# Tuned attention and MoE kernel: activation sums for two groups at a time in tiles 3 to 6, and another written order of tiles 1 to 6

## The chip, the cores and the metric

The kernel runs on one core of one Trainium2 chip. The metric is the device time of one execution in microseconds (us). Three runs of the kernel before gave 268.6, 267.94 and 268.05 us, so its median is 268.05 us. The profile was taken in one more execution of 268.22 us.

Five engines work side by side, each through a list of instructions of its own, in the order of that list: TensorE (PE; its weight loads are PEld), VectorE (DVE), ScalarE (ACT), GpSimd (POOL) and SyncE (SP), which here only issues DMAs. An instruction starts when the engine is free and the semaphores that it waits for have come.

## The reference, cut to what matters

Linear attention is followed by a two-layer network with a leaky ReLU:

```python
q_s = exp(q - max(q, axis=-1)); q_s = q_s / sum(q_s, axis=-1)      # q, k, v: (8, 8, 576, 64)
k_s = exp(k - max(k, axis=2));  k_s = k_s / sum(k_s, axis=2)
kv  = einsum('bhsd,bhse->bhde', k_s, v)
x   = einsum('bhsd,bhde->bhse', q_s, kv)                           # as (4608, 512)
h   = x @ w_in                                                     # w_in: (512, 2048)
out = maximum(0.01 * h, h) @ w_out                                 # w_out: (2048, 512)
```

## The kernel before, in words

The 4608 rows of x are nine tiles of 512 rows (tiles 0 to 8), and they come from eight batches of 576 rows (batches 0 to 7). Batch b has to be through the attention before the tile that uses its rows begins. So the attention of a batch runs beside the network of an earlier tile.

**Layer 1.** In tiles 1 to 5 it is a plain product: a word `u` in the order makes 4 matmuls, weights from `w_in_sb`, into a bank of PSUM (`ph`, line 516), and a word `l` lets ACT take the bank through the leaky ReLU into `gj` (line 525). In tiles 6 to 8 it is a scheme with seven products (`m1` to `m7`, line 918) where ACT and DVE take sums in between.

**Layer 2.** From tile 1 on it has seven products (`P1` to `P7`, line 948, bank `acc`) instead of eight. Four of them need sums of activations instead of activations: `n0` to `n3`, differences made on DVE (line 1005) and kept in the tiles `gs`. `P5` needs `n0`, `P6` needs `n1`, `P7` needs `n2` and `P3` needs `n3`; `n1` and `n3` are made from `n0` and `n1`. The activations of a tile stand in four groups p = 0 to 3. In the tiles named in `PAIRED`, one DVE instruction makes a sum for two groups (a half of the tile, 1024 elements to a partition); in the others there is one for each group (512 elements). In `PAIRED = (1, 2)` these are tiles 1 and 2; tiles 3 to 8 go by single groups. Between the products ACT copies a bank aside (`q1`, `q5`, `q6`: line 1015), and DVE adds it back at the end (`d11`, `d12`, `d22`: line 897). `w0` and `w1` issue the stores of a finished half tile on SP.

**The attention of a batch b.** `lk`, `lq`, `lv` issue loads on SP. `kt`, `km` take the maximum of k (DVE), `ks` subtracts it (DVE for batches 2 to 4, else POOL, line 193), `ke` takes exp (ACT, line 201), `va`, `vb` cast v (ACT, line 211), `kv` multiplies on PE (line 294), `kr` and `kd` scale the result. `qm` takes the maximum of q (DVE), `qs` subtracts it (POOL, line 256), `qe` takes exp (ACT, line 264), `qu` sums (DVE, line 273), `qn` divides (DVE, line 280), `qt` issues on SP a DMA that transposes (`qX`, line 457). Then `A` multiplies on PE (`po`, line 438), and `x` lets ACT copy a bank of that into `xT` (line 429), from which `u` or `m` read.

**What sets the order.** After tile 0 all of this is written out by hand, or by a search of its author, as one list of words, `SCORE`, which is played from left to right by `play`. Each word appends its instructions to the lists of its engines. The order of words therefore is the order on every engine, on SP's DMAs and POOL too; how far one engine runs ahead of another is left to the semaphores. A word that begins with a digit belongs to that tile: `5P200` is product 2 of tile 5, first block of 128 rows, first half of the sum, 4 matmuls; `5n0_1` is the second sum `n0` of tile 5. In the others the digit behind the letters is the batch: `A6.1` is the second part of `A` for batch 6, and `x6.10` copies the first of its two banks; `qn2.1` is the second part of the rows of batch 2. `SCORE` covers tiles 1 to 6 and batches 2 to 7. Tile 0 and batches 0 and 1 stand ahead of it, and tiles 7 and 8 follow it, in an order of their own (`WEAVE`). PSUM has six banks in the pool `psB` (`ph`, `po`, part of `acc`) and two in `psO`; a bank is given to the next user in turn once its last reader is through.

Line numbers are those of the kernel before. In the changed kernel all lines behind `SCORE` are two lower (948 is 946, 1005 is 1003, 1015 is 1013).

Of the kernel before, what the change touches and what calls it, by code (L numbers as in the profile page):

```python
# [25 lines left out]
def kernel(  # L26
# [759 lines left out]
    def xsums(t, steps=slice(0, 4)):  # L786
# [13 lines left out]
        1u13 1u02 kt2.1 kt2.2 kt2.3 1u00 1u01 1l00 1l02 1l13 1u03 1l03 lk3 1u06 1u10 qm2.1 qs2.1 qm2.0 1l01  # L800
        km2 lq3 1l06 qe2.1 qu2.1 1u04 1l04 1l10 1u12 1u07 ks2 qs2.0 qe2.0 qu2.0 1l12 1l07 1u11 1u15 1P100
        1l11 1u17 1n0_0 va2 1u05 1l05 1u14 1u16 1P101 1n1_0 ksB2 1l15 1l14 1l17 1l16 1P110 1P111 1P200 1n0_1
        1q1 qn2.0 1P201 qt2.0 1n1_1 qn2.1 qt2.1 1P500 1P501 1P510 1P511 1n2_0 1P600 1P601 1P610 1P611 T3
        1P210 vb2 1n2_1 1P211 lv3 1n3_0 ke2 kv2 1q6 1P700 1P701 kr2 1q5 1P710 1P711 1P300 lq4 1n3_1 1P301
        1d11 kd2 A2.0 x2.01 A2.1 x2.10 x2.00 x2.11 A2.2 kt3.0 1P310 1P311 1d22 1P400 1P401 kt3.1 kt3.2 x2.20
        1P410 qm3 1P411 x2.21 2u06 kt3.3 2u02 va3 vb3 2u04 2l04 2l06 km3 2u00 2l00 2u01 lq6 2l02 2l01 2u03
        1q21 qs3 2l03 qm4 lk5 2u17 qe3 2l17 2u10 2l10 2P100 2u07 2l07 ks3 1d12 2u12 lk4 2u05 2l05 2u14 2l12
        2u13 2u16 1w1 2l13 2u11 2u15 2P101 2l16 2l11 qs4 qu3 2P110 ksB3 2l14 2P111 2P200 2l15 qn3 2P201 ke3
# [1 line left out]
        2n2_0 qt3 2P510 2P511 kt4.0 2n2_1 2d11 2P700 lv4 2P701 2P710 A3.0 kt4.1 A3.1 2q5 2n3_0 qe4 x3.10  # L810
        A3.2 2P711 2P300 2n3_1 2P301 2P310 x3.01 2P311 kt4.2 2d22 x3.21 2P400 2P401 2P410 kt4.3 km4 ks4
        x3.20 2P411 x3.11 x3.00 3u06 3u04 3u17 2q21 3u15 3u07 va4 3l04 vb4 3l06 3l17 ksB4 3l15 3l07 3u00
        3l00 3u02 3u01 ke4 kt5.0 kt5.1 kt5.2 kt5.3 km5 ks5 3u13 3u11 kv4 3l02 3l13 3l01 3l11 3u05 3l05 kr4
        3u16 2d12 3u10 kd4 lv6 3u03 3l03 lq5 qu4 3l16 3u12 qn4 3l12 3n0_1 3u14 3l14 lk6 3n0_3 3l10 3n0_0
        3n0_2 3n1_1 3n3_1 lv5 va5 3P100 3P101 3P110 3P111 3q1 3P200 3P201 3P210 3P211 2w1 3P500 3P501 vb5
        qt4 3n1_2 3P510 3P511 3n1_0 3n1_3 3n3_0 2w0 3n3_2 3P600 3P601 3P610 3n2_3 3q5 3n3_3 3P611 3n2_1 3d11
        ke5 3P300 3q6 kt6.0 3P301 3P310 A4.0 A4.1 3n2_0 A4.2 kv5 kt6.1 3n2_2 kt6.2 lq7 qm5 3P311 3P700 x4.01
        x4.00 lk7 x4.20 kt6.3 3P701 3P710 3P711 x4.11 x4.21 x4.10 4u13 3d12 va6 4u02 4l02 4u12 4u03 3d22 vb6
        3P400 3P401 qs5 3P410 3P411 kr5 kd5 4l13 4u07 4l03 4l12 km6 4u06 4u00 4u17 qe5 4l06 4l17 qu5 4l07
# [10 lines left out]
        6m1_1 X6.0 Z0 X6.1 X6.2 5P710 5P210 X6.3 Z1 5P711 5d22 qe7 6s1_1 4w1 5P211 5d11 6m5_1 kd7 qu7 qn7  # L830
        6m1_2 6s1_2 5P400 5P401 5P410 5P411 5q21 6m1_0 6s1_0 Z2 6m1_3 6m6_1 6m6_2 6s1_3 6s6_1 6s6_2 6m6_0
        6m2_1 6c11_1 6m7_1 6s6_0 6s5_1 6m5_2 6s5_2 5P301 5P310 5P311 6l11_1 6c22_1 6m6_3 6l22_1 6m3_1 5d12
        6m4_1 6c12_1 6m2_2 6m3_2 6m2_3 6s6_3 6c11_2 6l21_1 6l12_1 qt7 6c11_3 6l11_2 6m5_3 6m5_0 6s5_3 6s5_0
        6m2_0 6c11_0 6m7_3 6l11_3 6c22_3 6m7_2 6c22_2 6l11_0 6m7_0 6l22_3 6m3_3 6m3_0 6c22_0 6m4_3 6l22_2
# [310 lines left out]
```

## Time and profile before

| | us |
|---|---|
| median of three runs (267.94 to 268.6) | 268.05 |
| profiled execution, its own time | 268.22 |
| span of its trace | 266.4 |
| PE busy (96%) | 256.3 |
| DVE busy (84%) | 224.6 |
| ACT busy (72%) | 193.0 |
| POOL busy (24%) | 64.3 |

The span goes from the first instruction to the last; 1.8 us of the execution's own time lie around it. The busy time of PE counts matmuls with modelled ends, so that it tells whether PE ever waited, and not how fast it went; how fast it went is to be read from the time that a number of equal matmuls took. The chain of waits is followed back from the last instruction, and its pieces are given in the order of time: start, length, engine, tile and line, and how many instructions. The view of groups gives, by line and shape, how many instructions there are, their busy time, and the mean of one.

### The profile page before, as it was taken

The page shows a single profiled execution, that of the slowest core. Times are in us where ns is not written, and L with a number is a line of the kernel's source. Part 1 is how long each engine was busy: PE and PEld are TensorE (multiplying, and loading weights), DVE is VectorE, ACT ScalarE, POOL GpSimd, SP SyncE. Part 2 cuts the span into 40 slices and gives each one's busy share as a digit, 9 for nine tenths or more (in the row PEclk, how much of TensorE's full clock was granted, in tenths as well). Part 3 has the DMA queues.
Part 4 walks back from the last instruction along what each step waited for, and adds up shares of the span by engine and source line. Part 5 has one row for each costly group of instructions (what it writes and reads, how often), then busy time and mean ns, then how long its engine had stood idle before and what let it go on. Part 6 is the DMA issues. An engine that isn't in the chain of part 4 may idle for free.

```text
span 266.4 us, 6323 instructions
## 1 busy us (share of the span) xinstructions
PE 256.3 (96%) x2570; PEld 188.6 (71%) x2570; DVE 224.6 (84%) x390; ACT 193.0 (72%) x367; POOL 64.3 (24%) x45
## 2 busy tenths in 40 slices
...
PEclk9999999999999999999999999999999999999999
...
GB/s 228 349 211 355 319 211 276 321 309 259 181 397 391 179 264 347 181 258 147 310 72 27 229 93 2 31 209 11 17 209 25 14 184 41 2 88 72 1 2 159
DMA packets 37646, 46.49 MB, mean 174 GB/s; under 512 B 18160, under 2 KB 21232, under 8 KB 37616
## 3 DMA queue, kind: packets, MB, share of 16 engines
...
## 4 chain that ended last, share of the span: by engine, by line
PE 85%; DMA 6%; ACT 2%; DVE 1%; issue 0%; POOL 0%; ACTq 0%; POOLq 0%
PE acc L948 37%; PE ph L516 29%; PE ph L918 14%; DMA w_in_sb<-in_moe_w_in_dram 3%; DMA qX<-qe 3%; PE po L438 2%; PE pkv L294 1%; ACT ke L201 1%; DVE k_raw L380 1%; PE pout L541 1%; PE po L294 1%; ACT vb L211 1%; ACT qe L264 0%; POOL w_in_sb L129 0%; DVE out_sb L897 0%
## 5 line engine op out<-in xcount | busy, mean ns | idle before, releaser
L516 PE MATMUL ph<-xT,w_in_sb 128*128 128x256 bf16 (+3 forms) x512 | 86.0, 326 | 0.5 <-DMA w_in_sb<-in_moe_w_in_dram 0.5
L516 PEld LDWEIGHTS <-w_in_sb 128*128 128x128 bf16 x512 | 49.7, 98 | 33.0 <-DMA w_in_sb<-in_moe_w_in_dram 0.8
L525 ACT ACTIVATE gj<-ph 128x512 bf16<-128x512 f32 (+2 forms) x116 | 60.7, 579 | 14.8 <-PE ph L516 11.7
L948 PEld LDWEIGHTS <-gs 128*128 128x128 bf16 x512 | 49.5, 98 | 6.2 <-issue 0.4
L256 POOL TENSOR_TENSOR q_raw<-q_raw,qmax 128x2304 f32<-128x2304 f32 (+3 forms) x10 | 31.0, 3104 | 62.5 <-DVE qmax L225 48.8
L948 PEld LDWEIGHTS <-gj 128*128 128x128 bf16 x384 | 37.4, 98 | 6.3 <-issue 0.5
L948 PE MATMUL acc<-w_out_sb,gj 128*128 128x256 bf16 x256 | 32.2, 273 | 0.0
L948 PE MATMUL acc<-w_out_sb,gs 128*128 128x256 bf16 x256 | 30.8, 273 | 0.0
L948 PE MATMUL acc<-wsum,gs 128*128 128x256 bf16 x256 | 29.9, 273 | 0.0
L897 DVE TENSOR_TENSOR part_spare<-ph,part_spare 128x512 f32<-128x512 f32 x36 | 23.8, 686 | 3.9 <-PE ph L918 3.6
L1005 DVE TENSOR_TENSOR gs<-gj 128x512 bf16<-128x512 bf16 (+1 forms) x56 | 24.3, 455 | 2.0 <-ACT gj L525 1.6
L429 ACT CAST xT<-po 128x512 bf16<-128x512 f32 (+3 forms) x47 | 19.0, 486 | 9.3 <-PE po L438 9.2
L982 ACT COPY part_spare<-ph 128x512 f32<-128x512 f32 x36 | 19.5, 594 | 8.3 <-PE ph L918 8.0
L1005 DVE TENSOR_TENSOR gs<-gj,gs 128x512 bf16<-128x512 bf16 (+1 forms) x56 | 24.1, 458 | 0.5
L280 DVE TENSOR_TENSOR qe<-qe,qrec 128x2304 bf16<-128x2304 bf16 (+4 forms) x12 | 23.7, 1973 | 0.2
L273 DVE TENSOR_REDUCE qsum<-qe 128x36 f32<-128x2304 bf16 (+4 forms) x11 | 19.7, 1793 | 4.6 <-ACT qe L264 4.6
L1015 ACT COPY keep<-acc 128x512 f32<-128x512 f32 x22 | 12.8, 588 | 11.7 <-PE acc L948 11.7
L193 POOL TENSOR_TENSOR k_raw<-k_raw,kall 128x2304 f32<-128x2304 f32 x3 | 15.2, 5064 | 24.2 <-DVE kall L185 24.2
L897 DVE TENSOR_TENSOR out_sb<-acc,keep 128x512 f32<-128x512 f32 (+1 forms) x26 | 16.4, 642 | 5.0 <-PE acc L948 3.7
L918 PEld LDWEIGHTS <-fs_spare 128*128 128x128 bf16 x192 | 18.8, 98 | 2.2
L225 DVE TENSOR_REDUCE qmax<-q_raw 128x36 f32<-128x2304 f32 (+4 forms) x11 | 19.5, 1790 | 0.4 <-DMA q_raw<-in_q_dram 0.4
L918 PE MATMUL ph<-xs_spare,fs_spare 128*128 128x256 bf16 x144 | 19.0, 273 | 0.0
...
## 6 DMA issues: line engine op xcount, KB each, us to landing
...
```

What stands on the lines that cost most here:

```text
L225: nc.vector.tensor_reduce(out=m, in_=st[b]["q"][:, :, rs], axis=AX.X, op=ALU.max)
L256: eng.tensor_tensor(out=qs, in0=qs, in1=st[b]["qmax", rs.start].unsqueeze(3).to_broadcast([P, HL, n, D]), op=ALU.subtract,)
L273: nc.vector.reduce_sum(out=qsum, in_=st[b]["qe"][:, rs], axis=AX.X)
L280: eng.tensor_tensor(out=qes, in0=qes, in1=st[b]["qrec", rs.start].unsqueeze(3).to_broadcast([P, n, HL, D]), op=ALU.mult,)
L429: eng.copy(out=o, in_=i)
L516: nc.tensor.matmul(ph[:, n0:n1], lhsT=w_in_sb[:, i, j * P : (j + 1) * P], rhs=xT[:, i, (c0 + n0) % NX : (c0 + n0) % NX + n1 - n0], start=( ...
L525: nc.scalar.activation(out=o, in_=ph, func=AF.Prelu, alpha=LEAKY_SLOPE)
L897: nc.vector.tensor_tensor(out=o, in0=x, in1=y, op=ALU.add)
L918: nc.tensor.matmul(bank[x, t, p][:, jj], lhsT=lhs(k, 2 * p + jj), rhs=rhs[:, k], start=(first and k == 0 and jj == 0), stop=(k == 1), skip ...
L948: nc.tensor.matmul(b[:, at_], lhsT=lhs(k)[:, sub * P : (sub + 1) * P], rhs=rhs[:, k], start=(first and k == 0 and at_ == 0), stop=(k % (NK ...
L982: nc.scalar.copy(out=fill(t, kind, p), in_=bank["Z" if kind == "s5" else "X", t, p])
L1005: nc.vector.tensor_tensor(out=o, in0=x, in1=y, op=ALU.subtract)
```

## The change

1. `PAIRED` takes in tiles 3 to 6. There the sums `n0` to `n3` are made for a half tile each: 8 instructions of 1024 elements in a tile, in place of 16 of 512. The code for it (`corners`, `place`) was there for tiles 1 and 2.
2. `SCORE` is another list. It has 699 words in place of 731: the 32 words of single sums that fall away are `n0_2`, `n0_3` and so on in tiles 3 to 6; all other words are the same, in another order.

Nothing else differs. Which engine does which work, the products, the loads, the stores, tile 0, and tiles 7 and 8 are as before.

```diff
-    PAIRED = (1, 2)
+    PAIRED = (1, 2, 3, 4, 5, 6)
     SCORE = """
...
-        2n0_0 2P210 2n0_1 2P211 2n1_0 2n1_1 2P500 kv3 2q1 2P600 2P601 2P610 2P611 2q6 kr3 kd3 1w0 2P501
...
-        4q1 4P510 4n2_0 4P600 4n3_3 4P601 4P610 4P611 ke6 4P511 4q6 4n3_2 kt7.1 A5.0 x5.01 A5.1 x5.00 4n2_1
-        A5.2 kv6 x5.20 x5.21 kt7.2 4n3_1 4n3_0 4n2_3 4n2_2 4P700 4P701 4P710 4P711 qm6 4q5 4P300 qm7 x5.10
-        x5.11 4P301 4P310 4P311 4d22 4P200 4P201 kr6 kd6 4P210 qs6 qs7 kt7.3 qe6 5u02 5l02 4P211 4P400 4P401
...
-        5q1 3w1 5n1_0 5n3_0 5P500 5n1_2 5P501 5P510 5P511 5P600 5P601 F1 ke7 5q5 A6.0 x6.01 A6.1 x6.00 F3
-        5n3_2 A6.2 kv7 5P610 5P611 x6.11 F2 F4 5q6 5n3_3 5P200 x6.20 5P300 5P201 5P700 5P701 x6.21 kr7 x6.10
...
-        6c12_3 6n1_1 6l12_0 6n0_0 6n1_0 6l12_2 6n0_2 6l12_3 6n0_3 6n2_3 A7.0 x7.00 A7.1 x7.11 6P210 6n1_3
...
-        6w0 A7.2 x7.20 6P400 6P401 6P410 x7.21 X7.0 X7.1 X7.2 6P411 6q21 6w1 X7.3 5w0
...
+        1l17 1l03 1u14 1l14 1u16 1l16 ksB2 1P100 qu2.0 qn2.0 1P101 1P110 1P111 1P200 ke2 1P201 1P210 1n0_0
+        1n0_1 qn2.1 1P500 1P501 1P510 1n1_0 lq3 1n1_1 1P211 va2 qt2.0 1q1 1P511 1P600 vb2 1q5 1n3_0 kv2
+        1P601 qt2.1 1P300 1n2_0 kr2 1P610 1P611 1n3_1 1P301 1d11 kd2 A2.0 A2.1 A2.2 1P310 1q6 x2.01 x2.00
...
+        2n2_0 kd3 2P601 kt4.0 kt4.1 2P610 2q5 2P611 lk6 A3.0 A3.1 2n3_1 A3.2 2q6 2P300 x3.20 x3.10 x3.01
...
+        3u05 3u14 3l05 kv4 kr4 kd4 3l14 3P100 3u13 3l13 3u15 3u16 3l16 qn4 lq6 3P101 3P110 lv6 3l15 3P200
+        2w0 qt4 3P111 3P201 3n0_0 3n0_1 3P210 3P211 3n1_1 3n1_0 3P500 3P501 3P510 3P511 3q1 3P600 3n3_1
...
+        4P610 4P611 4q6 qt5 A5.0 A5.1 A5.2 4q5 x5.10 kv6 qm6 x5.11 x5.01 3w0 qs6 4P700 4P701 4P710 4P711
+        x5.00 x5.21 4P300 4P301 4P310 4d22 km7 x5.20 4P200 4P201 4P210 va7 vb7 kr6 kd6 4P400 4P401 4P211
+        4P410 4P411 5u00 5l00 5u02 5l02 5u01 5l01 qe6 4d11 5u06 ks7 4P311 F1 qm7 5u12 qs7 5u07 5l06 5l07
+        4q21 qu6 4w1 4d12 5l12 5u03 5l03 5u10 ke7 5u05 5u04 5l04 5u16 qn6 3w1 5l10 5l16 5l05 5u13 5l13 5u15
+        5u11 5l11 5u17 5l17 5n0_0 5u14 5n2_0 5l15 5P100 5P101 5P110 5P111 5n2_1 5l14 5n0_1 5P500 5P501 5q1
+        5P510 5n1_0 5P600 5n1_1 5P601 5P610 5n3_1 5P611 5q6 qt6 A6.0 x6.00 A6.1 x6.10 A6.2 F2 x6.01 kv7
+        x6.20 5P200 x6.21 5P511 x6.11 5P700 5q5 qe7 5P701 5P201 5P210 5P710 5P211 5P711 F3 F4 5n3_0 X6.0 Z0
...
+        6n1_1 6P600 6P501 6P510 6l21_3 6P601 6P610 6l21_2 6n2_0 6P611 A7.0 A7.1 6q6 A7.2 6P511 x7.20 6P700
```

More of the change, by code (lines that the diff above doesn't have):

```diff
@@ L799 @@
     SCORE = """
[L800 to L808, printed above, removed]
-        2n0_0 2P210 2n0_1 2P211 2n1_0 2n1_1 2P500 kv3 2q1 2P600 2P601 2P610 2P611 2q6 kr3 kd3 1w0 2P501
@@ L810 @@
[L810 to L819, printed above, removed]
@@ L820 @@
-        4n0_1 4u04 4l00 ks6 qn5 4u16 4l16 kt7.0 4u01 4l01 4n0_3 4n1_3 3q21 4u14 4l04 4u11 4l11 4u05 4l05
-        4u10 4u15 4l10 4n0_0 4n1_0 4l15 4P100 4P101 qt5 4l14 4n0_2 4n1_2 4P110 4P111 4n1_1 4P500 4P501 lv7
-        4q1 4P510 4n2_0 4P600 4n3_3 4P601 4P610 4P611 ke6 4P511 4q6 4n3_2 kt7.1 A5.0 x5.01 A5.1 x5.00 4n2_1
-        A5.2 kv6 x5.20 x5.21 kt7.2 4n3_1 4n3_0 4n2_3 4n2_2 4P700 4P701 4P710 4P711 qm6 4q5 4P300 qm7 x5.10
-        x5.11 4P301 4P310 4P311 4d22 4P200 4P201 kr6 kd6 4P210 qs6 qs7 kt7.3 qe6 5u02 5l02 4P211 4P400 4P401
@@ L825 @@
-        3w0 4P410 va7 km7 4P411 5u01 5u06 5l06 5u04 5u00 5l00 5l01 4d11 5u16 vb7 5u10 5l04 qu6 4d12 5l16 ks7
-        5u11 qn6 5u17 5l10 4q21 5l11 5n0_0 5l17 5u03 5l03 5u12 5u05 5l05 5n2_2 5l12 5u13 5l13 5n0_1 5n1_1
-        5P100 5n3_1 5u07 5l07 5n0_3 qt6 5u15 5n2_3 5n2_1 5l15 5u14 5l14 5n1_3 5n0_2 5n2_0 5P101 5P110 5P111
-        5q1 3w1 5n1_0 5n3_0 5P500 5n1_2 5P501 5P510 5P511 5P600 5P601 F1 ke7 5q5 A6.0 x6.01 A6.1 x6.00 F3
-        5n3_2 A6.2 kv7 5P610 5P611 x6.11 F2 F4 5q6 5n3_3 5P200 x6.20 5P300 5P201 5P700 5P701 x6.21 kr7 x6.10
@@ L830 @@
[L830 to L834, printed above, removed]
@@ L835 @@
-        6c12_0 6l21_3 6m4_2 6l21_2 6c12_2 6m4_0 6l22_0 6P100 6P101 6P110 6P111 6l21_0 6P200 6P201 6n0_1
-        6c12_3 6n1_1 6l12_0 6n0_0 6n1_0 6l12_2 6n0_2 6l12_3 6n0_3 6n2_3 A7.0 x7.00 A7.1 x7.11 6P210 6n1_3
-        6q1 6n3_1 x7.10 6P500 6P501 6n2_0 6P510 6n1_2 6P511 6q5 6n2_1 6P600 6P601 6n3_2 6n3_0 6P610 6n3_3
-        6P611 4w0 6P211 6q6 6n2_2 6P300 6P301 6d11 x7.01 6P700 6P701 6P710 6P711 6P310 6P311 5w1 6d22 6d12
-        6w0 A7.2 x7.20 6P400 6P401 6P410 x7.21 X7.0 X7.1 X7.2 6P411 6q21 6w1 X7.3 5w0
+        1u00 1l00 1u11 1u10 1l10 1l11 1u02 1u04 1u15 kt2.1 kt2.2 kt2.3 1u05 qm2.1 1u12 1l02 qs2.1 qm2.0 1u07
@@ new lines @@
+        1l04 1l15 km2 1u06 qe2.1 1l05 1u13 1l12 qu2.1 qs2.0 qe2.0 1u03 ks2 lk3 1l13 1u01 1l06 1l07 1l01 1u17
+        1l17 1l03 1u14 1l14 1u16 1l16 ksB2 1P100 qu2.0 qn2.0 1P101 1P110 1P111 1P200 ke2 1P201 1P210 1n0_0
+        1n0_1 qn2.1 1P500 1P501 1P510 1n1_0 lq3 1n1_1 1P211 va2 qt2.0 1q1 1P511 1P600 vb2 1q5 1n3_0 kv2
+        1P601 qt2.1 1P300 1n2_0 kr2 1P610 1P611 1n3_1 1P301 1d11 kd2 A2.0 A2.1 A2.2 1P310 1q6 x2.01 x2.00
+        1P311 x2.20 T3 lq4 1P700 1n2_1 x2.21 1P701 lv3 1P710 1P711 x2.11 kt3.0 kt3.1 kt3.2 kt3.3 qm3 x2.10
@@ new lines @@
+        2u02 2l02 2u12 2l12 2u03 2l03 2u06 2u00 qs3 1d22 1P400 1P401 1P410 va3 vb3 2l00 2l06 qm4 qe3 km3
+        1d12 2u14 lk4 1w0 1P411 qs4 2u04 2l04 2u13 2l14 2u01 2l01 2u11 2u07 2l13 qu3 lv4 2u15 2u05 2l11 1q21
+        2l05 2l15 2u17 2l17 2l07 ks3 2u10 2l10 2u16 2P100 qn3 2P101 qt3 lk5 2l16 ksB3 ke3 2P200 2n0_0 2n0_1
+        2P201 2P210 2P211 2n1_0 2P110 2P111 2q1 2n2_1 2n1_1 2P500 2P501 2d11 2P510 kv3 kr3 2P600 2n3_0 2P511
+        2n2_0 kd3 2P601 kt4.0 kt4.1 2P610 2q5 2P611 lk6 A3.0 A3.1 2n3_1 A3.2 2q6 2P300 x3.20 x3.10 x3.01
@@ new lines @@
+        kt4.2 2P700 2P701 2P710 x3.21 1w1 2P711 2P301 2P310 lq5 2P311 x3.11 kt4.3 x3.00 3u02 3l02 2d22 km4
+        2P400 ks4 va4 2P401 2P410 2P411 3u00 qe4 ksB4 kt5.0 kt5.1 kt5.2 2q21 lv5 kt5.3 km5 ks5 vb4 3l00 3u06
+        3u03 3l03 3u07 qu4 3l06 3u17 3l17 3u01 3l01 2d12 3u11 3l07 3l11 3u10 ke4 3l10 3u04 3l04 3u12 3l12
+        3u05 3u14 3l05 kv4 kr4 kd4 3l14 3P100 3u13 3l13 3u15 3u16 3l16 qn4 lq6 3P101 3P110 lv6 3l15 3P200
+        2w0 qt4 3P111 3P201 3n0_0 3n0_1 3P210 3P211 3n1_1 3n1_0 3P500 3P501 3P510 3P511 3q1 3P600 3n3_1
@@ new lines @@
+        3n3_0 2w1 3P601 kt6.0 va5 vb5 3P610 3q5 ke5 3P611 3d11 3P300 3P301 3P310 A4.0 A4.1 3q6 A4.2 kv5
+        3n2_0 3n2_1 x4.00 x4.01 3P311 x4.20 x4.11 kt6.1 3P700 3P701 3P710 3P711 x4.21 x4.10 4u03 lq7 va6
+        kt6.2 kt6.3 qm5 4u13 4u02 3d22 qs5 3P400 3P401 3P410 vb6 3P411 4l02 4l13 kr5 kd5 3d12 4l03 4u12 4l12
+        4u10 4u00 qe5 4u06 4l06 4l00 4l10 4u16 4u17 4u05 4u01 km6 lk7 qu5 qn5 ks6 4l16 3q21 4u04 4l17 4l04
+        4l05 4u07 kt7.0 4l07 4u11 4u15 4l01 4l11 4n0_0 4u14 4l15 4l14 4n0_1 4P100 4P101 4P110 4P500 4P111
@@ new lines @@
+        4q1 4n2_0 4n1_0 lv7 4n1_1 4n2_1 kt7.1 4n3_1 kt7.2 ke6 4P501 4P510 4n3_0 4P511 4P600 kt7.3 4P601
+        4P610 4P611 4q6 qt5 A5.0 A5.1 A5.2 4q5 x5.10 kv6 qm6 x5.11 x5.01 3w0 qs6 4P700 4P701 4P710 4P711
+        x5.00 x5.21 4P300 4P301 4P310 4d22 km7 x5.20 4P200 4P201 4P210 va7 vb7 kr6 kd6 4P400 4P401 4P211
+        4P410 4P411 5u00 5l00 5u02 5l02 5u01 5l01 qe6 4d11 5u06 ks7 4P311 F1 qm7 5u12 qs7 5u07 5l06 5l07
+        4q21 qu6 4w1 4d12 5l12 5u03 5l03 5u10 ke7 5u05 5u04 5l04 5u16 qn6 3w1 5l10 5l16 5l05 5u13 5l13 5u15
@@ new lines @@
+        5u11 5l11 5u17 5l17 5n0_0 5u14 5n2_0 5l15 5P100 5P101 5P110 5P111 5n2_1 5l14 5n0_1 5P500 5P501 5q1
+        5P510 5n1_0 5P600 5n1_1 5P601 5P610 5n3_1 5P611 5q6 qt6 A6.0 x6.00 A6.1 x6.10 A6.2 F2 x6.01 kv7
+        x6.20 5P200 x6.21 5P511 x6.11 5P700 5q5 qe7 5P701 5P201 5P210 5P710 5P211 5P711 F3 F4 5n3_0 X6.0 Z0
+        X6.1 X6.2 X6.3 kr7 6m5_0 6s5_0 6m5_1 Z1 5d22 6m1_0 5P300 5P301 5P400 6s5_1 kd7 5P401 6m1_2 6m1_1
+        6s1_1 5P410 5d11 5P411 6s1_0 5P310 qu7 qn7 qt7 5P311 6m1_3 6s1_2 6m6_2 6m6_0 5q21 Z2 6s6_2 6m2_0 4w0
@@ new lines @@
+        6s6_0 6s1_3 5d12 6c11_0 6l11_0 6m3_0 6c12_0 6m2_1 6m6_1 6c11_1 6m6_3 6s6_1 6m3_1 6m5_3 6c12_1 6s6_3
+        6m2_3 6c11_3 6l11_1 6m7_1 6c22_1 6l12_0 6s5_3 6m5_2 6s5_2 6m2_2 6c11_2 6l11_3 6l12_1 6m7_2 6l11_2
+        6c22_2 6l22_1 6m3_3 6c12_3 6m3_2 6l12_3 6m7_0 6c22_0 6l22_0 6l22_2 6m7_3 6P100 6c22_3 6P101 5w0
+        6m4_1 6m4_0 6l22_3 6P110 6P111 6c12_2 6l12_2 6m4_2 6n0_0 6n1_0 6q1 6l21_1 6m4_3 6l21_0 6P500 6n0_1
+        6n1_1 6P600 6P501 6P510 6l21_3 6P601 6P610 6l21_2 6n2_0 6P611 A7.0 A7.1 6q6 A7.2 6P511 x7.20 6P700
```

2 lines of the change are left out of this document (added).

## The prediction

> **What bounds the kernel now.** I read the page first, then the waits of PE, then the chain of waits in the order of time, then busy time by stage.
>
> ```profile
> PE 256.3 (96%) x2570; PEld 188.6 (71%) x2570; DVE 224.6 (84%) x390; ACT 193.0 (72%) x367; POOL 64.3 (24%) x45
> PEclk9999999999999999999999999999999999999999
> ```
>
> ```profile
> PE pout L343 <- POOL zero L105: 1.3, 1, 1.3
> ...
> PE po L438 <- DMA qX<-qe: 0.3, 1, 0.3
> ```
>
> ```profile
> 40.52 7.54 DMA qX<-qe
> ...
> 50.84 9.08 PE ph L516 x48
> ...
> 69.93 0.71 PE pkv L294 x72
> ...
> 112.92 0.84 PE pkv L294 x72
> ...
> 136.13 10.48 PE ph L516 x96
> ...
> 178.41 0.62 PE po L438 x16
> ...
> 202.46 0.40 PE po L438 x8
> 202.86 7.97 PE acc L948 x72
> 210.82 0.34 PE po L438 x8
> 211.16 1.85 PE acc L948 x16
> ...
> 227.86 9.61 PE acc L948 x88
> ...
> 261.96 0.42 DVE out_sb L897
> ```
>
> ```profile
> 54.00:80.00 26.00, 26.00 (x265) 17.90 (x262) 25.06 (x43) 20.53 (x37) 5.89 (x3) 1.00 0.88 284
> 140.00:165.00 25.00, 25.00 (x284) 19.95 (x282) 23.95 (x39) 17.86 (x31) 9.85 (x3) 1.00 0.36 93
> 165.00:190.00 25.00, 25.00 (x266) 18.19 (x265) 23.27 (x34) 20.78 (x38) 3.42 (x1) 1.00 0.32 68
> ```
>
> After the transpose that lands at 48.06 us, the chain is PE and nothing else until DVE's last sum at 261.96. In the waits of PE no row is left for that stretch: the last one is the 0.3 us for that same qX. The stage rows (columns: length, then busy us of PE, PEld, DVE, ACT, POOL, then the granted clock) have PE busy in all of 76 us at clock 1.00, though DVE is at 25.06 of 26 and 23.95 of 25.
>
> Busy is not yet "at full rate". So I divide: 9.61 us over 88 products of 256 columns is 109.2 ns each, 10.48 over 96 of `u` is 109.2 (tile 4, whose columns wrap, has its `u` cut to 256), and 9.08 over 48 of 448 columns is 189.2. The time per column is the same early and late, in tiles with much DVE work and with little. Hence PE runs at one fixed rate from 48 us on, and the only time beside it is at the switches between kinds of matmul (below). The Trainium skill ("TensorE: Matmul & The Clock Gate", section "Wait — 56ns, not 53.3ns?") gives N ÷ 2.4 GHz + about 2.5 ns from start to start, 109.2 ns at 256 columns by my arithmetic; the trace agrees.
>
> **The change, part by part.** *Paired sums.*
>
> ```profile
> L1005 DVE TENSOR_TENSOR gs<-gj 128x512 bf16<-128x512 bf16 x48 | 19.0, 418 | 1.8 <-ACT gj L525 1.6
> L1005 DVE TENSOR_TENSOR gs<-gj,gs 128x512 bf16<-128x512 bf16 x48 | 18.8, 420 | 0.4
> ...
> L1005 DVE TENSOR_TENSOR gs<-gj 128x1024 bf16<-128x1024 bf16 x8 | 5.3, 677 | 0.1
> L1005 DVE TENSOR_TENSOR gs<-gj,gs 128x1024 bf16<-128x1024 bf16 x8 | 5.3, 684 | 0.1
> ```
>
> ```profile
> 92.67 1.29 DVE L1005 TENSOR_TENSOR gs<-gj,gs 128x1024 bf16<-128x1024 bf16 x2
> ...
> 121.36 2.56 DVE L1005 TENSOR_TENSOR gs<-gj,gs 128x512 bf16<-128x512 bf16 x7
> ```
>
> 64 sums of 419 ns become 32 of about 681: 26.8 us of busy time become 21.8, so 5.0 less. Neighbours overlap, so what DVE's queue gains is less: seven singles take 2.56 us, 0.36 from start to start; two pairs take 1.29, 0.61 from start to start. 64 x 0.36 - 32 x 0.61 = 3.5 us, some 0.9 in each of tiles 3 to 6. All of it is hidden, since PE waits for DVE nowhere: on the path it is 0. Without that cover it would be worth 3.5 us. What a pair costs: it waits for the second group's activation and is ready 0.26 us later than one single. In tile 3 the products `3P210 3P211` (8 x 0.109 = 0.87 us) stand between the first pair and `3P500`, which reads it, so this is 0 too.
>
> *The new order, port and POOL.*
>
> ```profile
> 163.35 5.06 POOL L193 TENSOR_TENSOR k_raw<-k_raw,kall 128x2304 f32<-128x2304 f32 x1
> ```
>
> ```profile
> 117.54 2.56 DVE L280 TENSOR_TENSOR qe<-qe,qrec 128x2304 bf16<-128x2304 bf16 x1
> ...
> 165.76 5.07 DVE L280 TENSOR_TENSOR qe<-qe,qrec 128x2304 bf16<-128x2304 bf16 x1
> ```
>
> The same division of q takes 2.56 us alone and 5.07 beside a subtraction on POOL that ends at 168.41: it seems to begin only then. The order puts POOL's `ks7` ahead of `qs7` and DVE's `qn6` behind more work, so this 2.5 us may go. PE is busy in all of 165 to 190, so it is worth 0 on the path; a new collision would cost 2.5 us of DVE and reach PE only where less cover than that is left. The Trainium skill ("SBUF — State Buffer", section "Who interferes with whom") says that a VectorE instruction with two SBUF inputs and a GpSimd one that reads SBUF exclude each other for a whole instruction; the row agrees, and the rule prices nothing on PE.
>
> *Switches on PE.* This is what the order can take off the path. A change between full matmuls and the half-height ones of `A` and `kv` costs time: 72 products after a block of `A` take 7.97 us, 72 x 0.1092 is 7.86, so 0.11 follows each block. In batch 7 `A7.0 A7.1` and `A7.2` stand apart (0.40 + 0.34 + 0.11 + 0.10 = 0.95); now they stand together, as in batch 6 (0.62 + 0.11 = 0.73): 0.22 saved. `kv4` takes 0.84 where `kv2` takes 0.71: up to 0.13 saved, or nothing if its new place has the same. The other blocks stand apart or together as before. Sum -0.22 to -0.35.
>
> *Where cover is thin.* (a) Batch 6: now `5q6 A6.0 x6.00 A6.1 x6.10 A6.2 ... kv7 x6.20 5P200`. `A6` takes all six banks, so `5P200` needs the bank that `x6.00` empties, behind `5q6` on ACT.
>
> ```profile
> 178.38 0.58 ACT L1015 COPY keep<-acc 128x512 f32<-128x512 f32 x1
> 178.84 1.57 ACT L429 CAST xT<-po 128x512 bf16<-128x512 f32 x3
> ```
>
> ```profile
> 178.34 0.69 PE L438 MATMUL po<-qX,kd 64*64 64x512 bf16 x16
> 178.86 0.79 PE L294 MATMUL po<-vb,ke 64*64 64x65 bf16 x72
> 179.58 1.05 PE L948 MATMUL acc<-wsum,gs 128*128 128x256 bf16 x8
> ```
>
> The same work stands so in these rows: a copy, then three casts in 1.57 us, the first done at about 178.84 + 0.61 = 179.45, and PE is through `A` and `kv` at 179.58. 0.13 us are left; a wake-up of PE may eat that. I take 0.1 for it, with 0 and 0.4 (most of one more ACT instruction of 0.58) as ends.
>
> (b) DVE in tile 1, where pairs are nothing new and DVE gains nothing.
>
> ```profile
> 58.47 1.29 DVE L193 TENSOR_TENSOR k_raw<-k_raw,kall 128x1152 f32<-128x1152 f32 x1
> 59.69 1.47 DVE L273 TENSOR_REDUCE qsum<-qe 128x20 f32<-128x1280 bf16 x1
> 61.19 0.28 DVE L275 RECIPROCAL qrec<-qsum 128x20 f32<-128x20 f32 x1
> ...
> 64.84 1.49 DVE L280 TENSOR_TENSOR qe<-qe,qrec 128x1280 bf16<-128x1280 bf16 x1
> 66.24 0.68 DVE L1005 TENSOR_TENSOR gs<-gj,gs 128x1024 bf16<-128x1024 bf16 x1
> 66.84 1.22 DVE L280 TENSOR_TENSOR qe<-qe,qrec 128x1024 bf16<-128x1024 bf16 x1
> ```
>
> Now both `ks2`, `qu2.0` and `qn2.0` stand ahead of `1n0_0`. From 58.47: two subtractions 2 x 1.22, sum and reciprocal 1.70, division 1.40 (each from start to start), so `1n0_0` begins at 64.0 and is done at 64.7. PE: 64 `u` from 50.84 end at 62.95; with `P1` and three of `P2`'s four words, 28 x 0.109, `1P500` begins at 66.0. 1.3 us are spare. `1n0_1` (done 65.3) has until 66.9. So no wait.
>
> (c) The transposes. `qn2.1` then ends at 66.5; `A2` on PE comes at 62.95 + 72 x 0.109 + 0.82 for `kv2` = 71.6, so qX has 5.1 us.
>
> ```profile
> DMA to landing us min/median/max: 3.1/4.6/7.5
> ```
>
> It lands 3.1 to 7.5 us after its issue: at the median 0.5 are left, at the longest PE waits 2.4. I take 0: the 7.5 is the first one, at 40.5 us in the chain, and half of them land within 4.6. (d) SP's own order: loads and stores are the same in number, and `lv4` now stands behind the stores of `1w0`. Its reader `va4` comes behind more than 100 products of tile 2, over 11 us. ACT, POOL and SP have the same instructions: 0.
>
> **Sum.** Against the profiled execution: 268.22 - 0.3 + 0.1 = 268.0. That execution lies 0.17 above the median of 268.05, so the forecast for the median is 267.9.
>
> **Rivals.** *A transpose comes late* (slower). Place: `A2`, or another `A` moved forward; from a landing of 5.1 us after the division on, each us late is a us of PE. At 7.5 it gives 267.9 + 2.4 = 270.3. For it: the margin is 0.5 at the median. Against it: no transpose after 48 us kept PE waiting before, and from the old division's end (68.06) to the old `A2` (73.4) there were 5.3 us, as good as the same.
>
> *DVE's relief reaches the end* (faster). PE would have slack that busy time hides, and 3.5 us would show: 264.5. Against it: 109.2 ns everywhere. The Trainium skill ("Perfetto Trace Analysis", section "Identifying the Most-Contended Engine") warns that matmul busy time is a poor measure and points to the share of weight loads, which at 71% would leave room; here the time per matmul speaks against that.
>
> *The change does nothing that can be told.* That is the forecast's own neighbourhood: 0.3% is 0.8 us, about what a measurement tells from no change, and the whole sum is less.
>
> **How the numbers follow.** Forecast (PE bound, switches -0.35 to -0.22, waits 0 to 0.5): 0.78, within 0.3%. Late transposes, or a wait of their size elsewhere in a list that is new throughout: 0.15, slower. Relief shows: 0.05, and 0.02 for other gains: faster 0.07. Range: 267.9 less the rest of the gain and the spread of the runs, 267.3; upwards the bound of (a) and half of one late transpose, 269.0.
>
> **What would show it.** Right: PE's waits again end with qX before 50 us, the chain is PE to the last sum, PE's last matmul ends 0 to 0.4 us earlier, DVE's busy time is near 217 us (5 for pairs, 2.5 for the collision), no 5 us division at 166. Wrong: a PE row waiting for qX, `xT` or `gs` of over 0.5 us in 60 to 215, or fewer than 109 ns to a product.

## The result, and the profile after

The changed kernel took 269.1 us (median of five runs, 269.01 to 269.27), the kernel before 268.05 (five runs, 267.74 to 268.6). The ratio is 1.0038 with a 95% interval of 1.0024 to 1.0053: slower by about 1 us. The profiled execution of the changed kernel took 269.27 us with a span of 267.5.

The page of the changed kernel, busy time of the engines, and two rows of its waits of PE (waited for, us in total, times, longest):

```profile
PE 256.0 (96%) x2559; PEld 188.9 (71%) x2570; DVE 224.7 (84%) x358; ACT 192.8 (72%) x367; POOL 63.0 (24%) x45
```

```profile
PE acc L946 <- DVE gs L1003: 0.8, 1, 0.8
...
PE po L438 <- DMA qX<-qe: 0.3, 1, 0.3
```

DVE has 32 instructions fewer, as it should, and yet as much busy time as before (224.6). And PE has a wait that it did not have: once, on a sum of activations. The chain of waits of the changed kernel, in the order of time (start, length, engine, tile and line, how many), shows where:

```profile
50.69 12.11 PE ph L516 x64
...
95.17 0.84 PE pkv L294 x72
...
115.49 0.71 PE pkv L294 x72
...
152.99 5.80 PE acc L946 x52
...
158.81 0.69 DVE out_sb L895
159.50 5.95 DVE fs_spare L780
...
171.33 3.13 DVE qe L280
174.46 2.42 DVE gs L1003 x4
...
176.93 2.79 PE acc L946 x24
...
205.54 0.61 PE po L438 x16
206.16 7.53 PE acc L946 x68
...
228.53 9.61 PE acc L946 x88
...
262.63 0.42 DVE out_sb L895
```

Before, this chain was PE alone from 48 us to the last sum. Now it leaves PE at 158.8, goes over DVE for 18 us, and comes back to PE at 176.93. The first piece on DVE to look at is that of 5.95 us: `fs_spare`, the word `F1`. The words `F1` to `F4` make, on DVE, four differences of blocks of `w_in` which tile 6 needs later (128 x 2048, both inputs in SBUF). Rows of DVE in the changed kernel (start, length, the idle time before in brackets):

```profile
159.42 6.04 DVE L780 TENSOR_TENSOR fs_spare<-w_in_sb 128x2048 bf16<-128x2048 bf16 x1
165.38 2.54 DVE L225 TENSOR_REDUCE qmax<-q_raw 128x36 f32<-128x2304 f32 x1
...
171.25 3.21 DVE L280 TENSOR_TENSOR qe<-qe,qrec 128x2304 bf16<-128x2304 bf16 x1
174.38 2.48 DVE L1003 TENSOR_TENSOR gs<-gj 128x1024 bf16<-128x1024 bf16 x4
...
179.85 1.22 DVE L780 TENSOR_TENSOR fs_spare<-w_in_sb 128x2048 bf16<-128x2048 bf16 x1
```

and of POOL in the changed kernel at the same time:

```profile
155.30 4.05 POOL L256 TENSOR_TENSOR q_raw<-q_raw,qmax 128x2304 f32<-128x2304 f32 x1 [15.46 <-DVE qmax L225]
159.31 5.07 POOL L193 TENSOR_TENSOR k_raw<-k_raw,kall 128x2304 f32<-128x2304 f32 x1
...
168.00 4.05 POOL L256 TENSOR_TENSOR q_raw<-q_raw,qmax 128x2304 f32<-128x2304 f32 x1 [3.62 <-DVE qmax L225]
```

The same shape takes 1.22 us at 179.85 and 6.04 us at 159.42. POOL's subtraction for k (`ks7`) begins at 159.31, 0.11 us ahead of `F1`, and ends at 164.38; `F1` ends 1.08 us after that. So `F1` looks held for the whole of POOL's instruction, and loses 4.8 us. The division of q (`qn6`, 171.25) is held in the same way, until POOL's `qs7` ends at 172.05, and takes 3.21 where 2.56 is its time alone: 0.65 more. DVE's four pairs for tile 5 therefore come late, and PE stops in the middle of `P5`:

```profile
175.48 0.60 PE L946 MATMUL acc<-wsum,gs 128*128 128x256 bf16 x4
...
176.93 2.79 PE L946 MATMUL acc<-wsum,gs 128*128 128x256 bf16 x24 [0.85 <-DVE gs L1003]
```

Busy time in the stretch (length, then busy us of PE, PEld, DVE, ACT, POOL, then the granted clock, the DMA share and GB/s) of the changed kernel,

```profile
157.00:178.00 21.00, 20.05 (x121) 11.72 (x121) 20.14 (x19) 14.72 (x25) 11.42 (x3) 1.00 0.34 74
```

and of the kernel before:

```profile
157.00:178.00 21.00, 21.00 (x132) 12.71 (x131) 19.65 (x33) 16.20 (x26) 11.42 (x3) 1.00 0.28 58
```

PE lacks 0.95 us of 21, at the same clock. The views of waits give 0.8 and 0.85, because they count from the modelled end of the product before. By starts, the four products at 175.48 would be through at 175.48 + 4 x 0.109 = 175.92, and the next begins at 176.93, so 1.01 us are lost. The rest of the sum is small. From the first `u` after the transpose to DVE's last sum the changed kernel takes 262.63 - 50.69 = 211.94 us, the kernel before 261.96 - 50.84 = 211.12, so 0.82 more: 1.01 for the wait, less some 0.2 that PE gained elsewhere. Before that stretch 0.15 us are gained, and behind it, from the start of the last sum to the end of the span, it is 4.9 us in place of 4.4. Together 0.82 - 0.15 + 0.4, the 1.1 by which the span is longer.

### The profile page after: what moved, and what is told of

Read it like the earlier page. It is cut to its first block, busy times and chain, and to the rows that moved or that the text cites. A ratio compares the mean times of both kernels' runs of the same rounds, so it can differ in the third digit from the quotient of the medians.

```text
span 267.5 us, 6287 instructions
## 1 busy us (share of the span) xinstructions
PE 256.0 (96%) x2559; PEld 188.9 (71%) x2570; DVE 224.7 (84%) x358; ACT 192.8 (72%) x367; POOL 63.0 (24%) x45
## 4 chain that ended last, share of the span: by engine, by line
PE 78%; DVE 8%; DMA 6%; ACT 2%; issue 1%; POOL 0%; ACTq 0%; POOLq 0%
PE acc L946 36%; PE ph L516 24%; PE ph L916 14%; DMA w_in_sb<-in_moe_w_in_dram 3%; DMA qX<-qe 3%; DVE fs_spare L780 2%; PE po L438 2%; DVE qe L280 1%; DVE qsum L273 1%; DVE qmax L225 1%; DVE gs L1003 1%; PE pkv L294 1%; ACT ke L201 1%; PE po L294 1%; DVE k_raw L380 1%; PE pout L541 1%
## 5 line engine op out<-in xcount | busy, mean ns | idle before, releaser
L256 POOL TENSOR_TENSOR q_raw<-q_raw,qmax 128x2304 f32<-128x2304 f32 (+3 forms) x10 | 29.7, 2975 | 65.5 <-DVE qmax L225 65.5
L946 PE MATMUL acc<-wsum,gs 128*128 128x256 bf16 x256 | 30.9, 273 | 0.8 <-DVE gs L1003 0.8
L1003 DVE TENSOR_TENSOR gs<-gj 128x1024 bf16<-128x1024 bf16 (+1 forms) x40 | 22.1, 577 | 1.3 <-ACT gj L525 1.3
L280 DVE TENSOR_TENSOR qe<-qe,qrec 128x2304 bf16<-128x2304 bf16 (+4 forms) x12 | 22.4, 1864 | 0.3
L1003 DVE TENSOR_TENSOR gs<-gj,gs 128x1024 bf16<-128x1024 bf16 (+1 forms) x40 | 22.2, 577 | 0.3
```

The lines of the kernel that those rows point to most:

```text
L256: eng.tensor_tensor(out=qs, in0=qs, in1=st[b]["qmax", rs.start].unsqueeze(3).to_broadcast([P, HL, n, D]), op=ALU.subtract,)
L280: eng.tensor_tensor(out=qes, in0=qes, in1=st[b]["qrec", rs.start].unsqueeze(3).to_broadcast([P, n, HL, D]), op=ALU.mult,)
L946: nc.tensor.matmul(b[:, at_], lhsT=lhs(k)[:, sub * P : (sub + 1) * P], rhs=rhs[:, k], start=(first and k == 0 and at_ == 0), stop=(k % (NK ...
L1003: nc.vector.tensor_tensor(out=o, in0=x, in1=y, op=ALU.subtract)
```

## The experiments

The theory after the result (theory 1): the loss is `F1` held by POOL's `ks7`; pairs and the rest of the order cost nothing. Its rivals: the pairs themselves make PE wait, since each needs two activations; or something else in the new order does. Each kernel was compared with the kernel before on the same chip, in five rounds; the kernel before had medians of 267.76 us (e1 to e4), 267.77 (e5, e6) and 267.64 (e7 to e9). In the table, "F1 against ks7" says by how much `F1` was asked after (+) or before (-) POOL's `ks7` began, "PE's new waits" are those of the view of waits, and "stretch" is the time from the first `u` to the last sum, read from the chain as above (before 211.12, after 211.94).

| run | median, us | ratio (95%) | F1 against ks7, us | F1 took, us | PE's new waits, us | stretch, us |
|---|---|---|---|---|---|---|
| changed kernel | 269.1 | 1.0038 (1.0024 to 1.0053) | +0.11 | 6.04 | 0.8 | 211.94 |
| e1 F1 late | 267.81 | 0.9999 (0.9991 to 1.0008) | far behind | 1.22 | none | 210.85 |
| e2 F1 early | 267.82 | 1.0002 (0.9993 to 1.0011) | -1.25 | 2.38 | none | 210.80 |
| e3 old order, pairs | 269.3 | 1.006 (1.0047 to 1.0072) | far behind | 1.22 | 0.7 | 212.22 |
| e4 singles, F1 late | 267.93 | 1.0008 (0.9999 to 1.0017) | far behind | 1.22 | none in the view (0.24, see e4) | 211.14 |
| e5 singles | 267.8 | 0.9998 (0.9989 to 1.0007) | -0.38 | 1.50 | none | 210.87 |
| e6 n0 first | 268.55 | 1.0031 (1.002 to 1.0041) | +0.11 | 6.04 | 0.6 | 211.69 |
| e7 kr6 ahead | 267.96 | 1.0006 (0.9998 to 1.0015) | -0.45 | 1.57 | none | 210.88 |
| e8 singles, qm6 early | 272.19 | 1.0173 (1.0159 to 1.0187) | +0.50 | 5.65 | 2.7 + 1.1 | 215.16 |
| e9 F1 behind qm7 | 267.88 | 1.0008 (0.9999 to 1.0017) | +2.56 | 3.59 | none | 210.86 |

### e1: F1 moved behind the collision

```diff
-  ... ks7 4P311 F1 qm7 ... x6.10 A6.2 F2 x6.01 ...
+  ... ks7 4P311 qm7 ... x6.10 A6.2 F1 F2 x6.01 ...
```

> The changed kernel with one word moved: F1, the first sum of weights on DVE, stands ahead of F2 (behind A6.2) instead of ahead of qm7. Theory 1 (F1 met POOL's subtraction of k and held DVE for 6.04 us instead of 1.22; the wait of PE of 1.0 us in tile 5 is its consequence): the subtraction on POOL runs beside qm7, F1 takes about 1.2 us, DVE's sums of tile 5 are some 4.8 us earlier, the 1.0 us wait is gone and the time is 269.1 - 1.0 = 268.1, within 0.2 of the kernel before. Theory 2 (the pairs themselves are late, because a pair needs the second group's activation and 5n0_1 stands behind both 5n2): the wait stays, 269.1.

267.81 us, ratio 0.9999. One word moved, and the whole loss is gone. Ends of the chain of e1 (its first row is cut off at 56 us):

```profile
50.67 5.49 PE ph L516 x29
...
261.52 0.42 DVE out_sb L896
```

DVE of e1, with the idle time before in brackets:

```profile
159.33 2.54 DVE L225 TENSOR_REDUCE qmax<-q_raw 128x36 f32<-128x2304 f32 x1
164.83 2.55 DVE L273 TENSOR_REDUCE qsum<-qe 128x36 f32<-128x2304 bf16 x1 [2.96 <-ACT qe L264]
...
172.75 2.53 DVE L1004 TENSOR_TENSOR gs<-gj 128x1024 bf16<-128x1024 bf16 x4 [1.95 <-ACT gj L525]
...
177.13 1.22 DVE L780 TENSOR_TENSOR fs_spare<-w_in_sb 128x2048 bf16<-128x2048 bf16 x1
```

The maximum of q (`qm7`, 159.33), which has one input, runs beside POOL's `ks7` (159.22 to 164.29) and takes its usual 2.54: not every instruction of DVE is held. The rows also price the cover. Ahead of the four pairs DVE idles 2.96 + 1.95 = 4.91 us here. In the changed kernel `F1` (5.96 from its start to the next one's) and the longer `qn6` (0.65) are pushed into that stretch: 6.61 against 4.91, so the pairs should come 1.7 us late. They come at 174.38 in place of 172.75, 1.63 late, of which about 1.0 reached PE. The new order thus ends in the same time as the old one if `F1` doesn't collide, as the forecast had it.

### e2: F1 moved ahead of the sum of tile 4

```diff
-  ... 5l01 qe6 4d11 5u06 ks7 4P311 F1 qm7 ...
+  ... 5l01 qe6 F1 4d11 5u06 ks7 4P311 qm7 ...
```

> The changed kernel with F1 two places earlier on DVE's way, ahead of 4d11, so that it asks for its operands while POOL's subtraction of q (until 159.35 us) still runs and before that of k begins. Theory 1 leaves two ways: if who has waited longer goes first, F1 is held for about 1.2 us, runs to about 160.5, POOL's subtraction of k begins 1.2 us later, and the wait in tile 5 is gone: 268.1. If POOL goes on from one subtraction to the next, F1 is held until 164.4 with 4d11 behind it, and the time is 269.1 or more. Theory 2: 269.1 in either case.

267.82 us, ratio 1.0002. DVE of e2, and POOL of e2:

```profile
157.61 2.38 DVE L780 TENSOR_TENSOR fs_spare<-w_in_sb 128x2048 bf16<-128x2048 bf16 x1
```

```profile
154.85 4.05 POOL L256 TENSOR_TENSOR q_raw<-q_raw,qmax 128x2304 f32<-128x2304 f32 x1 [15.45 <-DVE qmax L225]
158.86 6.07 POOL L193 TENSOR_TENSOR k_raw<-k_raw,kall 128x2304 f32<-128x2304 f32 x1
```

`F1` is asked while POOL subtracts for q, and waits until that ends at 158.90. Then `F1` goes, though POOL has its next subtraction at hand, and now that one is held: 6.07 us instead of 5.07. So both engines block each other, and the one that waited goes first. PE noticed nothing.

### e3: pairs in the old order

```diff
-    PAIRED = (1, 2)
+    PAIRED = (1, 2, 3, 4, 5, 6)
-  ... 4l14 4n0_2 4n1_2 4P110 4P111 4n1_1 4P500 ... 4n3_0 4n2_3 4n2_2 4P700 ...
+  ... 4l14 4n0_1 4n1_1 4P110 4P111 4n1_0 4P500 ... 4n3_0 4n2_1 4P700 ...
```

Against the kernel before, whose order is kept; each pair stands where the later of its two singles stood.

> The kernel before with the pairs alone: tiles 3 to 6 by pairs, each pair where the later of its two singles stood, all other words in the old order. Theory 1: the pairs are hidden, 268.05 within 0.3, no new wait in tiles 3 to 6, DVE's busy time 5 us lower. Theory 2: a wait for a sum appears in tiles 3 to 6 as in the changed kernel, 268.6 or more.

269.3 us, ratio 1.006: slower by 1.5 us, and not the 268.05 of theory 1. The collision of `F1` is not in it. What it has is another wait of PE, in the waits and in the chain of e3:

```profile
PE acc L947 <- DVE gs L1004: 0.7, 2, 0.5
```

```profile
174.64 0.61 ACT gj L525
175.25 0.02 issue
175.27 1.91 DVE gs L1004 x3
...
177.20 1.30 DVE gs L1004 x2
...
178.55 0.61 PE acc L947 x4
```

An activation of tile 5 ends on ACT, DVE makes five pairs in a row, and PE waits for the last. In the old order there were places (this one, and one in tile 4) where a single sum could be made at once, while a pair has to wait for the second group. So in that order pairs do cost time, and the new order is not free to be judged by itself: it is what makes room for them. Of the 1.54 us the stretch carries 212.22 - 211.12 = 1.10. Measured from the first `u`, the block of `A` at 151.91 comes 0.35 later than in the kernel before (151.85 there) and that at 179.16 comes 1.04 later (178.41 there), so the two places, 0.35 and 0.69, are nearly all of it. The remaining 0.4 of the median lies outside the stretch and was not found in the trace of one execution.

### e4: single sums in the new order, F1 late

```diff
-    PAIRED = (1, 2, 3, 4, 5, 6)
+    PAIRED = (1, 2)
-  ... ks7 4P311 F1 qm7 ... 5l17 5n0_0 5u14 5n2_0 5l15 ... A6.2 F2 ...
+  ... ks7 4P311 qm7 ... 5l17 5n0_0 5n0_1 5u14 5n2_0 5n2_1 5l15 ... A6.2 F1 F2 ...
```

Two singles stand where each pair of tiles 3 to 6 stood, and `F1` stands as in e1.

> The new order with F1 ahead of F2 and single sums in tiles 3 to 6 (two singles where each pair stood). Theory 1: DVE has 0.9 us more to do in each tile, all hidden: the same time as with pairs and F1 ahead of F2, within 0.3 us. Theory 2: faster than the changed kernel because the pairs are gone, and faster than the run with pairs and F1 ahead of F2.

267.93 us, ratio 1.0008. It is e1 without the pairs, and the two can't be told apart by their intervals. The stretch is 211.14 against 210.85, so at most some 0.3 us of the pairs' 3.5 us of queue reach the end. The chain of e4 shows where: it leaves PE at 183.64 and goes over DVE to a sum in tile 6.

```profile
190.91 0.61 DVE out_sb L898
...
191.57 6.27 PE ph L919 x56
```

PE's four products at 190.89 would be through at 191.33 and the next begins at 191.57, so 0.24 us are lost, too little to stand in the view of waits. With `F1` late, the pairs are worth that much. With `F1` in its place they are worth nothing: the stretch is 210.87 in e5 and 210.88 in e7 below.

### e5: single sums in the new order, F1 in place

The edit is that of e4, but `F1` stays at `ks7 4P311 F1 qm7`.

> The changed kernel's order with F1 where it is, but single sums in tiles 3 to 6 (two singles where each pair stood). The collision of F1 stays. Theory 1 (the wait of 1.0 us in tile 5 is DVE's lateness after the collision): the two singles in place of each of the four pairs ahead of the awaited product take 8 x 0.36 = 2.9 us instead of 2.4, so the wait grows to about 1.4 us and the time is 269.4 to 269.6. Theory 2 (pairs are what is late): the wait shrinks or goes, 268.6 or less.

267.8 us, ratio 0.9998: a miss. Theory 1 wanted the collision here too, with nothing to shorten DVE's queue. DVE of e5, and POOL of e5:

```profile
159.10 1.50 DVE L780 TENSOR_TENSOR fs_spare<-w_in_sb 128x2048 bf16<-128x2048 bf16 x1
```

```profile
159.48 6.06 POOL L193 TENSOR_TENSOR k_raw<-k_raw,kall 128x2304 f32<-128x2304 f32 x1
```

`F1` was there 0.38 us ahead of POOL, where in the changed kernel it came 0.11 behind. Measured from the first `u` (50.42 in e5), `F1` comes at 108.68 us, as in the changed kernel (108.73), but POOL's `ks7` at 109.06 where it was 108.62: the singles keep DVE longer ahead of `qm6`, on which POOL's two subtractions wait. So POOL was the one held, by 1 us, and PE doesn't need it here. `F1` ends at 160.60 and `ks7` at 165.54, so `F1` doesn't wait for a result of `ks7`; what makes one wait for the other is that they run at the same time. So the pairs do have a part in the loss, by accident: they shift a race. Two further runs, e7 and e8, test that reading.

### e7: the race turned with the pairs kept

```diff
-  ... kv6 qm6 x5.11 ... va7 vb7 kr6 kd6 ...
+  ... kv6 kr6 qm6 x5.11 ... va7 vb7 kd6 ...
```

A small reciprocal on DVE goes ahead of `qm6`, so that POOL begins a little later.

> The changed kernel, pairs and F1's place kept, with kr6 (two short reciprocals on DVE, which wait for kv6 until about 153.0 us) moved ahead of qm6. So qm6 and POOL's subtraction of q behind it come some 0.6 us later, while F1, which stands behind 4d11 and its wait for PE, keeps its time. Theory (the race for the port): POOL's subtraction of k then begins at about 159.9 instead of 159.3, F1 asks at 159.4 and comes first, takes 1.2 to 1.8 us instead of 6.0, POOL is held instead, the 1.0 us wait is gone: 267.8. If the order at the port is not what decides: 269.1.

267.96 us, ratio 1.0006. DVE of e7, and POOL of e7:

```profile
159.10 1.57 DVE L780 TENSOR_TENSOR fs_spare<-w_in_sb 128x2048 bf16<-128x2048 bf16 x1
```

```profile
159.55 6.06 POOL L193 TENSOR_TENSOR k_raw<-k_raw,kall 128x2304 f32<-128x2304 f32 x1
```

As expected. Pairs, order and the place of `F1` are those of the changed kernel; `F1` is 0.45 us ahead of POOL instead of 0.11 behind, and a microsecond is back (the stretch is 210.88 against 211.94). The division `qn6` is even held for longer here than in the changed kernel, 4.00 us (3.94 in e5) against 3.21, because more of POOL's `qs7` is left when it begins (1.59 us here, 0.80 there). `F1` (1.50 from start to start) and `qn6` (1.44 more than alone) together push 2.94 us into the 4.91 us in which DVE idles, and PE doesn't wait.

### e8: the race turned back with single sums

Against e5, two words more are moved, so that `qm6` is early again:

```diff
-  ... kt7.1 4n3_2 4n3_3 kt7.2 ke6 ... 4P600 kt7.3 4P601 ... kv6 qm6 x5.11 ...
+  ... kt7.1 4n3_2 4n3_3 ke6 ... 4P600 4P601 ... kv6 qm6 kt7.2 kt7.3 x5.11 ...
```

> The mirror image: the run with single sums and F1 in its place (267.8 us, F1 first at the port by 0.38 us), with kt7.2 and kt7.3 moved behind qm6, so that POOL's subtractions come 0.67 us earlier. Theory (the race): POOL's subtraction of k begins at about 158.8, F1 asks at 159.1 and is held for some 6 us again, and PE waits about 1 us in tile 5: 268.8 to 269.2. If single sums are what saved that run: 267.8 still.

272.19 us, ratio 1.0173: slower as expected, and by 3 us more than expected. Waits of PE, DVE and POOL of e8:

```profile
PE acc L949 <- DVE out_sb L898: 2.7, 1, 2.7
...
PE acc L949 <- DVE gs L1006: 1.1, 1, 1.1
```

```profile
155.01 4.15 DVE L160 TENSOR_TENSOR kmax<-t,k_raw 128x256 f32<-128x256 f32 x1
...
162.65 5.65 DVE L780 TENSOR_TENSOR fs_spare<-w_in_sb 128x2048 bf16<-128x2048 bf16 x1
```

```profile
154.78 4.10 POOL L256 TENSOR_TENSOR q_raw<-q_raw,qmax 128x2304 f32<-128x2304 f32 x1 [14.91 <-DVE qmax L225]
...
162.15 5.07 POOL L193 TENSOR_TENSOR k_raw<-k_raw,kall 128x2304 f32<-128x2304 f32 x1 [3.26 <-issue]
```

`F1` lost the race again (0.50 behind POOL) and PE waited 1.1 for the sums, as in the changed kernel. The other 2.7 us come from the word that was moved for the purpose: `kt7.3`, an instruction of 256 elements that takes 0.42 alone, was asked 0.23 after POOL had begun, and took 4.15. Behind it stands the sum `4d22`, whose bank PE needs. Nor is the second collision the race that the edit was to set up. POOL stood idle for 3.26 us before this `ks7`, because the maximum of k that it subtracts (`km7`, behind `kt7.3` on DVE) was done only at 162.02. The run thus shows twice that DVE is held, but it is no clean mirror image of e7, and the expected 268.8 to 269.2 stays untested.

### e6: the collision left, and n0 made first

```diff
-  ... 5n0_0 5u14 5n2_0 5l15 ... 5P111 5n2_1 5l14 5n0_1 5P500 ...
+  ... 5n0_0 5u14 5l15 ... 5P111 5l14 5n0_1 5n2_0 5n2_1 5P500 ...
```

> The changed kernel with F1 where it is, and the pairs 5n2_0 and 5n2_1, which only P7 reads, moved behind 5n0_1, which P5 reads first. The collision stays and F1 takes 6 us again; if the cost on PE is only DVE's lateness less the cover, 5n0_1 comes 2 x 0.6 = 1.2 us earlier, unless its own activation 5l14 holds it, the 1.0 us wait is gone with the collision still there, and the time is 268.1. If the collision costs PE in another way as well, 269.1 less at most a few tenths.

268.55 us, ratio 1.0031. Waits and PE of e6:

```profile
PE acc L947 <- DVE gs L1004: 0.6, 1, 0.6
```

```profile
176.85 2.09 PE L947 MATMUL acc<-wsum,gs 128*128 128x256 bf16 x16 [0.57 <-DVE gs L1004]
```

A part of what was expected. `F1` still takes 6.04, and PE gets `n0` ahead of two pairs that it needs later. The wait shrinks from 0.85 to 0.57 and no more, since `n1` then stands behind the two pairs that were moved. It agrees that DVE's lateness at the pairs is what PE pays for, and that a reorder of the pairs doesn't remove it.

### e9: a collision in idle time

```diff
-  ... ks7 4P311 F1 qm7 5u12 ...
+  ... ks7 4P311 qm7 F1 5u12 ...
```

> The changed kernel with F1 one word later on DVE, behind qm7. F1 still meets POOL's subtraction of k, in its middle (asks at about 161.9, held until 164.4, done at 165.5), but in a stretch where DVE waited for the exponential of q until 164.8 in the run with F1 ahead of F2. Theory: DVE is late by 0.7 us instead of 3.0 at qu6, which is inside the cover of tile 5: no wait, 267.8. If any collision costs PE: 268.5 or more.

267.88 us, ratio 1.0008. DVE of e9, and POOL of e9:

```profile
161.50 3.59 DVE L780 TENSOR_TENSOR fs_spare<-w_in_sb 128x2048 bf16<-128x2048 bf16 x1
```

```profile
158.94 5.07 POOL L193 TENSOR_TENSOR k_raw<-k_raw,kall 128x2304 f32<-128x2304 f32 x1
163.96 5.04 POOL L256 TENSOR_TENSOR q_raw<-q_raw,qmax 128x2304 f32<-128x2304 f32 x1
```

As expected. `F1` is held for 2.4 us, and POOL behind it for 1 us, but it falls into the 2.96 us in which DVE has nothing to do but wait for `qe` (the row of e1). A collision costs what is left of it after DVE's idle time, not what its row shows.

None of these kernels is faster than the kernel before by more than the intervals.

## Why the prediction was wrong

*PE bounds, 109.2 ns a product.* Right: 88 products take 9.61 us in the chain after as well. The stretch is 210.80 to 210.88 us in the five runs without a loss on PE (e1, e2, e5, e7, e9), and in the others of the new order it is longer by about what their traces show as lost.

*Paired sums, 0 on the path.* Right in the new order to 0.3 us (e1 against e4, e7 against e5), but for a reason that the prediction gave for one tile only. It looked at the 0.26 us that a pair is later in tile 3, found cover there, and put the wait for the second group's activation at nothing elsewhere. In the old order (e3) the same pairs lack that cover in tiles 4 and 5, and the stretch is 1.1 us longer. The cover belonged to the order, and was to be read tile by tile. In the changed kernel the pairs also turned the race of `F1` (e5), which no one could read from their price.

*Port and POOL: the step that failed.* The prediction knew the mechanism and had its row, the 5.07 us division at 165.76. It asked whether that known collision would go (it nearly did: `qn6` takes 3.21), and priced a new one at "2.5 us of DVE", 0 on the path. That had two faults. First, it named no place for a new one. The list says `ks7 4P311 F1 qm7`: an instruction of DVE with two inputs in SBUF right behind the word that gives POOL its next 5 us. Whether `F1` wins or loses there could not be read from the list to 0.1 us, but that it might lose could, and it deserved a rival of its own. Secondly, the price: what is lost is POOL's instruction as far as it has yet to run, up to 5.07 us for a subtraction of k and 4.05 for one of q; 2.5 was merely what was left of one in the row before. Measured: `F1` takes 5.96 us of DVE's queue in its new place (4.8 of it held) and `qn6` 0.65 more, less 4.91 of idle time, so the pairs are 1.7 late, and PE lost 1.0. With 2.5 in place of 4.8 the same sum is 4.3, less than the 4.91, and PE would not have waited: the size decides. By such a sum the forecast would have had a second case near 269; which of the two would come, the list could not tell. Another new collision fits the rest of the prediction: `qn4` takes 3.1 in every kernel of the new order where it took 2.56 before, beside a subtraction on POOL, and PE never waits for it. The Trainium skill ("SBUF — State Buffer", section "Who interferes with whom") has it that the engine that issues first keeps the shared port for its whole instruction, and that this, and not the shape, decides who is blocked; the runs agree (`F1` 6.04 when 0.11 behind, 1.50 when 0.38 ahead, and POOL 6.06 instead of 5.07).

DVE's busy time was to be 217; it was 224.7, and 219.4 in e1 without the collision. So 5.3 of the 7.7 us missing are `F1` and `qn6`. The other 2.4 were not followed up to the end; the 5.0 for the pairs adds durations that overlap (3.5 from start to start, as the prediction says itself), and `qn4` adds 0.54.

*Switches, -0.22 to -0.35.* `A7` in one block came as forecast: 0.61, and then 68 products in 7.53, 0.10 more than 68 x 0.1092, so 0.71 in place of 0.95. `kv4` takes 0.71 now, but `kv3` takes 0.84, so the other 0.13 only moved. With the collision away, the stretch is 210.85 in e1 and 211.12 before: -0.27. Yet the time of e1 is that of the kernel before: what stands ahead of the stretch and behind it differs by as much (50.84 before, 50.67 in e1, and 4.4 and 4.8 from the last sum's start to the end of the span). So the gain on PE is there in the traces, one execution of each, and it doesn't show in the time.

*Thin cover.* (a) to (d) made no wait: PE's waits after 50 us have one row, that on `gs`. (In (b) the reader of `1n0_1` is `1P501` and not the product behind it, so some 0.4 us of the spare time given there were not there; what was left sufficed.) The 0.1 for (a) was not needed. The rival of late transposes did not happen. "Or a wait of their size elsewhere in a list that is new throughout", 0.15, is what came, but it had neither a place nor a mechanism. The rival by which DVE's relief reaches the end fell: with 5.2 us less on DVE, e1 takes the time of the kernel before.

*The range* ended at 269.0, from (a) and half of one late transpose. Those terms do not give 269.0: 267.9, with 0.4 in place of the 0.1 and half of 2.4, is 269.4. That would have held 269.1, but by luck, since no transpose came late. A term for one POOL instruction at the port, up to 5.07 us less the idle time that can be shown, was missing.
